# Fused windowed attention and soft mixture of experts: two PSUM tiles for the second layer, first weight tiles cut across four experts, and another grouping of the output rows

## The chip, the cores and the metric

One core of one Trainium2 chip. The metric is the device time of one execution in microseconds (us); before the change it is 223.0 us, the median of three runs (222.9 to 223.66).

## The reference, cut to what matters

```python
x = attention(q, k, v)                # 4 sink keys + a window of 128; x: 3072 tokens x 512
logits = x @ phi                      # 512 -> 32 slots (8 experts x 4 slots)
d = softmax(logits, axis=0);  slot_input = d.T @ x          # 32 x 512
for e in range(8):                    # w1: 8 x 512 x 1024,  w2: 8 x 1024 x 512
    h = np.maximum(slot_input[e] @ w1[e], 0.0)
    slot_out[e] = h @ w2[e]
c = softmax(logits, axis=1)
return c @ slot_out                   # 3072 x 512, fp32
```

All is fp32. The change touches what follows the attention: the two expert layers and the last product.

## The kernel before, in words

A planner (`Plan`) writes down the attention part in an order that it works out from costs and keys. During that part most of the expert weights are loaded into a ring of 22 tiles of 1 MB (`slot()`, name `wt`; two more 1 MB places, `first`, take weights too). What follows, `Moe.tail`, is written out by hand, in program order on each engine, and all its DMAs are issued by SyncE in that order:

- **Layer 1** (lines 634 to 658). Two rounds `r` of four experts. `hp` is a pair of PSUM tiles, one for each half `f` of the 1024 hidden columns. For each quarter `k` of the 512 inputs the four experts' products (`j`, 32 rows of PSUM each) run for `f` = 0 and then for `f` = 1. A weight tile of kind 0 holds two experts' 1024 columns of one quarter, so each tile is read for both `f`. After `k` = 0 and `k` = 1 of each round `more(2)` issues two further weight loads; a load waits until TensorE has done with the tile whose place it takes.
- **Layer 2** (`second`, line 663). `second(r, h, k0, k1)` multiplies the hidden values of round `r` with column half `h` of `w2`. Both halves are summed in one PSUM tile, `op`, of two banks, one for each `h`. The last four loads are `w2` of experts 0 to 3, half 1 (kind 1), which only `second(0, 1)` reads, in turns of `j` = 0 to 3.
- **`split(h)`** (line 673). ScalarE (line 675) and then VectorE (line 676) turn a finished half of `op` into the two-part right operand `tw` of the last product.
- **`combine(h, parts)`** (line 682). The output is 12 row groups `n` (256 tokens each) by two column halves `h`: 24 pieces of 256 KB. A piece is two matmuls, one copy out of PSUM (line 691, ScalarE for even `n`, VectorE for odd) and its part of an output DMA (line 692); each pair in `parts` is one DMA. `combine(0, ...)` is run between parts of `second(1, 1)`, so that output can be written while half 1 is still being computed.

The framework makes an instruction wait by whole tiles: a matmul that writes a PSUM tile waits until what still reads that tile is done.

Of the kernel before, what the change touches and what calls it, by code (L numbers as in the profile page):

```python
# [8 lines left out]
F32 = mybir.dt.float32  # L9
# [10 lines left out]
P = 128  # L20
# [58 lines left out]
class Sinks:  # L79


    def __init__(self, nc, plan, pool, tmp, c, v, store):
# [35 lines left out]
        def project(e):  # L118
            for a in range(4):
                nc.tensor.matmul(M["tile"][:, 0:32], lhsT=per[:, a].rearrange("p b x -> p (b x)"), rhs=c.phi[:, a, :],  # L120
                                 start=(a == 0), stop=(a == 3))

        plan.add(9.5, "D", 2.0, load, w=["v4"])
        plan.add(1.0, "G", 0.6, clear, w=["swide", "vphi", "pst"])
        plan.add(1.0, "G", 0.15, lambda e: nc.gpsimd.tensor_copy(tmp[:, 64:128], v4), r=["v4"], w=["v4b"])
# [183 lines left out]
class Moe:  # L309
# [291 lines left out]
    def tail(self, slot, wts, more, out):  # L601
        nc, c, B, si, pool = self.nc, self.c, self.B, self.si, InOrder(self.pools)
        hs = ht = None

        def halves(o, src):
            for x in range(2):
                i = slice(64 * x, 64 * x + 64)
                nc.tensor.transpose(o[x], src[i], c.ident[i, i])

        def turned(r):  # L610
            tp = [pool.tile() for _ in range(2)]
            for k in range(8):
                halves([t[:, 64 * k:64 * k + 64] for t in tp], hs[:, r, k])
            for j in range(4):
                t, o = tp[j // 2].rearrange("p (k y) -> p k y", k=8), 8 * j + 4 * r + 32 * (j % 2)
                eng = nc.vector.tensor_copy if j % 2 else nc.scalar.copy
                eng(ht[:, :, r, j, :, 4 * r:4 * r + 4], t[:, :, o:o + 4].unsqueeze(2).to_broadcast([P, 8, 4, 4]))

        def turn():
            tp = [pool.tile() for _ in range(2)]  # L620
            for u in range(3):
                cf = self.cs[3, u][1].bitcast(F32).rearrange("p y q e i -> p (y q e i)")
                for i in range(2):
                    o = P * u + 64 * i
                    halves([t[:, o:o + 64] for t in tp], cf[:, P * i:P * i + P])
            for x in range(2):
                if self.sinks:
                    o = self.ct[3][:, :, x].rearrange("p u (i y) -> p u i y", i=2)
                else:
                    o = self.ct[3][:, :, :, 64 * x:64 * x + 64]  # L630
                (nc.scalar.copy if x else nc.vector.tensor_copy)(
                    o, tp[x][:, 0:3 * P].rearrange("p (u i y) -> p u i y", u=3, i=2))

        for r in range(2):
            hp = [pool.tile() for _ in range(2)]
            for k in range(4):
                if r == 1 and k == 3:
                    turned(0)
                for f in range(2):
                    for j in range(4):  # L640
                        o = j % 2 * 1024 + 512 * f
                        nc.tensor.matmul(hp[f][32 * j:32 * j + 32, :], lhsT=si[:, k, :],
                                         rhs=wts[0, 4 * r + j // 2 * 2, k][:, o:o + 512],
                                         start=(k == 0), stop=(k == 3))
                if k < 2:
                    more(2)
            if r == 0:
                hs = slot().rearrange("p (r k m) -> p r k m", r=2, k=8)
                ht = slot().rearrange("p (k r j q i) -> p k r j q i", k=8, r=2, j=4, q=4)
                nc.gpsimd.memset(ht, 0.0)  # L650
            o, (h0, h1) = hs[:, r].rearrange("p k m -> p m k"), (h.rearrange("p (m k) -> p m k", k=8) for h in hp)
            nc.scalar.activation(o[:, 0:64], h0, AF.Relu, scale=self.rz)
            nc.vector.tensor_scalar(o[:, 64:128], h1, 0.0, self.rz, op0=ALU.max, op1=ALU.mult)
            if r == 0:
                self.place(slot(), [3], 3)
                more(1)
                for u in range(3):
                    self.stack(pool, 0, 3, u)

        op = pool.tile("s")[:, :, 0:256]  # L660
        tw = slot().bitcast(F32R)[:, 0:1024].rearrange("p (x m) -> p x m", x=2)

        def second(r, h, k0=0, k1=8):
            for k in range(k0, k1):
                for j in range(4):
                    if r:
                        w = wts[2, 4 + j, k // 4][:, 512 * (k % 4) + 256 * h:512 * (k % 4) + 256 * h + 256]
                    else:
                        w = wts[1, j, h][:, 256 * k:256 * k + 256]
                    nc.tensor.matmul(op[32 * j:32 * j + 32, h], lhsT=ht[:, k, r, j].rearrange("p q i -> p (q i)"), rhs=w,  # L670
                                     start=(r == h and k == 0), stop=(r == 1 - h and k == 7), skip_group_check=True)

        def split(h):
            hi = tw[:, 0, 256 * h:256 * h + 256]
            nc.scalar.copy(hi, op[:, h])  # L675
            nc.vector.scalar_tensor_tensor(tw[:, 1, 256 * h:256 * h + 256], hi.bitcast(F32), c.lo_rows, op[:, h],  # L676
                                           op0=ALU.mult, op1=ALU.add)


        ov = out.rearrange("(n p) m -> p n m", p=P)  # L680

        def combine(h, parts):
            o = slice(256 * h, 256 * h + 256)
            for n0, n1 in parts:
                ob = slot()[:, 0:512 * (n1 - n0)].rearrange("p (n m) -> p n m", m=256)
                for n in range(n0, n1):
                    yp = pool.tile().rearrange("p (i m) -> p i m", i=2)
                    for i in range(2):
                        nc.tensor.matmul(yp[:, i], lhsT=self.ct[n // 3][:, n % 3, i, :], rhs=tw[:, 1, o],
                                         start=(i == 0), stop=(i == 1), skip_group_check=True)  # L690
                    (nc.vector.tensor_copy if n % 2 else nc.scalar.copy)(ob[:, 2 * (n - n0):2 * (n - n0) + 2], yp)  # L691
                nc.sync.dma_start(ov[:, 2 * n0:2 * n1, o], ob)

        second(0, 0, 0, 4)
        turned(1)
        second(0, 0, 4, 8)
        turn()
        second(1, 0)
        split(0)

        second(1, 1, 0, 2)

        combine(0, ((0, 1), (1, 2), (2, 4)))
        second(1, 1, 2, 3)
        combine(0, ((4, 7),))
        second(1, 1, 3, 4)
        combine(0, ((7, 10),))
        second(1, 1, 4, 8)
        second(0, 1)
        split(1)  # L710
        combine(0, ((10, 12),))
        combine(1, ((0, 1), (1, 2), (2, 4), (4, 8), (8, 12)))


class Weights:


    def __init__(self, nc, w1, w2):
        self.nc, self.w1, self.w2, self.tiles, self.at = nc, w1, w2, [], {}
        first = [(0, 4 * r + 2 * j, k) for r in range(2) for k in range(4) for j in range(2)]  # L720
        self.order = first[:8] + [(1, e, 0) for e in range(4)] + first[8:]
        self.order += [(2, e, h) for h in range(2) for e in range(4, 8)] + [(1, e, 1) for e in range(4)]

    def load(self, t):
        kind, e, h = self.order[len(self.tiles)]
        if kind == 0:
            t2, w = t.rearrange("p (k m) -> p k m", k=2), self.w1[e:e + 2].rearrange("e (k p) m -> p e k m", p=P)[:, :, h, :]
        elif kind == 2:
            t2, w = t.rearrange("p (k m) -> p k m", k=4), self.w2[e].rearrange("(p k) m -> p k m", p=P)[:, 4 * h:4 * h + 4]
        else:  # L730
            t2 = t.rearrange("p (k m) -> p k m", k=8)
            w = self.w2[e].rearrange("(p k) m -> p k m", p=P)[:, :, 256 * h:256 * h + 256]
        self.nc.sync.dma_start(t2, w)
        self.tiles.append(t)
        self.at[kind, e, h] = t
# [50 lines left out]
def window_path(ctx, tc, c, moe, q, k, v, phi, w1, w2, out):  # L786
# [299 lines left out]
    for n, (b, j) in enumerate(jobs):  # L1086
# [3 lines left out]
        for kind in range(2):  # L1090
            for i in range(2):
                load(t(O["load"][kind]), n, kind, i)
            prep(t(O["prep"][kind]), n, kind)
        for i in range(2):
            load(t(O["v"][i]), n, 2, i)
# [266 lines left out]
```

## Time and profile before

| | |
|---|---|
| median of three runs | 223.0 us |
| profiled execution | 224.03 us, its span 222.3 us |
| TensorE busy | 201.1 us, 90% of the span |
| layer 1 starts | 171.15 us |
| half 0 of layer 2 complete | 194.3 us |
| half 1 complete (`split(1)` starts) | 206.36 us |
| last copy out of PSUM ends | 212.35 us |

All times are of the profiled execution's span. The 1.7 us between the span and the execution's time lie outside the span. Read first what the DMA engines do in the tail (share and GB/s by stretch), then the chain of waits there.

### The profile page before, as it was taken

How to read it: one execution, taken by the hardware profiler on the slowest of the kernel's cores; microseconds unless marked ns; L12 is line 12 of the kernel's file. 1: busy time of each engine (PE TensorE's matmuls, PEld its weight loads, DVE VectorE, ACT ScalarE, POOL GpSimd, SP SyncE). 2: the span in 40 equal slices, each digit the busy share in tenths (PEclk: the TensorE clock that was granted, in tenths of full speed). 3: DMA queues.
4: the chain of work that ended last, by engine and by line, in shares of the span. 5: the costliest groups of instructions: out<-in, count | busy, mean ns of one | idle time of the engine just before them, and what ended most of it. 6: DMA issues, size and time to landing. Idle time of an engine off the chain costs nothing.

```text
span 222.3 us, 9076 instructions
## 1 busy us (share of the span) xinstructions
PE 201.1 (90%) x3595; PEld 143.8 (65%) x3595; DVE 161.2 (73%) x459; ACT 146.0 (66%) x582; POOL 129.6 (58%) x247
## 2 busy tenths in 40 slices
PE   7977999998999999999999999998999999989800
PEld 6855787776777776776777777766777335555600
DVE  3778898798999989999987989999866123142710
ACT  2456699998888889788998889798445013141600
POOL 5069598877787796578887767877735240000000
PEclk9999999999999999999999999999999999999995
DMA  5998989898999979999999999994479999999696
GB/s 129 222 187 162 177 192 268 209 274 206 220 277 220 336 179 333 245 212 272 219 344 197 261 208 351 382 403 168 191 249 378 379 420 388 356 353 379 225 330 202
DMA packets 95829, 59.47 MB, mean 268 GB/s; under 512 B 76324, under 2 KB 90660, under 8 KB 94756
## 3 DMA queue, kind: packets, MB, share of 16 engines
q1 hardware_dynamic: 95776, 58.83, 91.2%
q8 instruction: 30, 0.49, 1.0%
q14 instruction: 19, 0.16, 0.2%
q10 hardware_dynamic: 4, 0.00, 0.0%
HBM read 52.53 MB, written 6.29 MB: 265 GB/s over the span
## 4 chain that ended last, share of the span: by engine, by line
PE 60%; DVE 15%; ACT 10%; issue 6%; POOL 5%; POOLq 0%; ACTq 0%; DVEq 0%
PE w L155 41%; PE s L155 17%; ACT wt L155 8%; DVE s L155 5%; DVE wt L155 5%; POOL wt L155 5%; DVE sums L155 2%; PE w L1314 2%; DVE rs L155 1%; DVE first L155 1%; DVE acc L155 1%; ACT wt L691 1%; DVE wt L676 0%; ACT wt L675 0%; DVE wt L691 0%
## 5 line engine op out<-in xcount | busy, mean ns | idle before, releaser
L155 ACT ACTIVATE wt<-s,wt 128x132 f32<-128x132 f32 x192 | 68.9, 380 | 9.4 <-DVE wt L155 6.4
L155 POOL TENSOR_TENSOR wt<-wt 128x528 f32<-128x528 f32 x46 | 49.3, 1073 | 18.4 <-DVE wt L155 7.9
L155 POOL TENSOR_SCALAR_AFFINE_SELECT wt<-wt 128x512 f32<-128x512 f32 x84 | 51.1, 636 | 7.4 <-ACT wt L155 3.8
L155 PE MATMUL w<-wt 128*64 128x128 f32 (+2 forms) x548 | 49.9, 316 | 1.9 <-POOL wt L155 1.4
L155 PE MATMUL s<-wt,qt 64*64 64x196 f32 (+2 forms) x768 | 43.0, 326 | 2.4 <-ACT wt L155 1.4
L155 PEld LDWEIGHTS w<-wt 128*64 128x64 f32 (+1 forms) x548 | 35.6, 140 | 14.4 <-POOL wt L155 3.8
L155 ACT ACTIVATION_READ_ACCUMULATOR wt<-s,wt 128x1 f32 x192 | 41.3, 215 | 0.0
L155 DVE TENSOR_REDUCE wt<-s 128x4 f32<-128x528 f32 x48 | 34.0, 708 | 1.7
L155 ACT COPY wt<-w 128x512 f32<-128x512 f32 (+2 forms) x39 | 21.8, 558 | 15.0 <-PE w L155 12.1
L155 PE MATMUL w<-ident,wt 64*128 64x64 f32 (+1 forms) x569 | 28.7, 231 | 1.9 <-POOL wt L155 1.0
L155 PEld LDWEIGHTS s<-wt,qt 64*64 64x64 f32 x768 | 25.4, 133 | 7.6 <-ACT wt L155 2.3
L155 PEld LDWEIGHTS w<-ident,wt 64*128 64x128 f32 (+1 forms) x569 | 22.2, 139 | 10.4 <-issue 4.3
L155 DVE COPY wt<-w 128x512 f32<-128x512 f32 (+2 forms) x36 | 22.8, 654 | 5.4 <-PE w L155 5.0
L155 ACT COPY first<-w 128x512 f32<-128x512 f32 x37 | 21.4, 596 | 3.6 <-PE w L155 3.2
L155 DVE COPY_PREDICATED s<-later,s 128x256 f32<-128x256 uint8 x48 | 20.3, 423 | 2.3 <-PE s L155 1.8
L155 PE MATMUL w<-ident,first 64*128 64x64 f32 x448 | 20.8, 232 | 0.3 <-DVE acc L155 0.2
L155 PEld LDWEIGHTS w<-ident,first 64*128 64x128 f32 x448 | 16.6, 141 | 6.6 <-issue 3.2
L155 PE MATMUL s<-wt 128*32 128x256 f32 x240 | 15.9, 381 | 1.0 <-DVE wt L676 1.0
L155 PE MATMUL w<-wt,si 128*32 128x512 f32 x120 | 14.1, 593 | 0.0
L155 PEld LDWEIGHTS s<-wt 128*32 128x32 f32 x240 | 7.8, 110 | 7.4 <-DVE wt L676 1.5
L155 DVE TENSOR_SCALAR wt<-wt 128x6 f32<-128x6 f32 x48 | 11.5, 240 | 0.7 <-ACT wt L155 0.3
L155 POOL COPY sk<-wt 128x16 f32<-128x16 f32 x48 | 9.4, 208 | 4.2 <-PE w L155 2.6
(134 smaller groups left out, 252.3 us busy)
## 6 DMA issues: line engine op xcount, KB each, us to landing
wt<-in_moe_w_dram SPq DMA_DIRECT2D x30, 1024.0 KB, 8.5
wt<-in_v_dram SPq DMA_DIRECT2D x24, 256.0 KB, 4.4
first<-in_q_dram SPq DMA_DIRECT2D x14, 256.0 KB, 4.3
first<-in_k_dram SPq DMA_DIRECT2D x14, 256.0 KB, 4.6
wt<-in_k_dram SPq DMA_DIRECT2D x8, 256.0 KB, 4.9
wt<-in_q_dram SPq DMA_DIRECT2D x8, 256.0 KB, 5.0
first<-in_moe_w_dram SPq DMA_DIRECT2D x2, 1024.0 KB, 7.0
out_dram<-wt SPq DMA_DIRECT2D x2, 1024.0 KB
```

The source lines that it names most:

```text
L155: return self.tc.keep_in_program_order(f(*args, **kw))
L691: (nc.vector.tensor_copy if n % 2 else nc.scalar.copy)(ob[:, 2 * (n - n0):2 * (n - n0) + 2], yp)
L1314: nc.tensor.matmul(t[:, 0:P], lhsT=c.ident, rhs=c.ident, start=True, stop=True)
```

## The change

Three edits, all in `Moe.tail` and `Weights`:

1. `op` becomes two PSUM tiles, one for each half.
2. The first two weight tiles change their cut: kind 3 holds four experts' quarter `k` = 0 for one half `f` (512 columns each, 2 KB runs) in place of two experts' 1024 columns (4 KB runs). So `f` = 0 reads only the first of them, and a load is issued after each `f`, one and one, in place of two after both. The number of loads and their order behind are as they were (`more(2)` at the three later points).
3. `combine(0, ...)`: four row groups, then 4-6, 6-8 (before: 4-7, 7-10) between the parts of `second(1, 1)`. Behind `split(1)` come 8-10, then half 1's first four, then half 0's 10-12, then half 1's 4-8 and 8-12 (before: half 0's 10-12, then half 1).

```diff
                 for f in range(2):
                     for j in range(4):
                         o = j % 2 * 1024 + 512 * f
-                        nc.tensor.matmul(hp[f][32 * j:32 * j + 32, :], lhsT=si[:, k, :],
-                                         rhs=wts[0, 4 * r + j // 2 * 2, k][:, o:o + 512],
+                        w = wts[3, 0, f][:, 512 * j:512 * j + 512] if r + k == 0 else wts[0, 4 * r + j // 2 * 2, k][:, o:o + 512]
+                        nc.tensor.matmul(hp[f][32 * j:32 * j + 32, :], lhsT=si[:, k, :], rhs=w,
                                          start=(k == 0), stop=(k == 3))
-                if k < 2:
+                    if r + k == 0:
+                        more(1)
+                if 0 < r + k < 3 and k < 2:
                     more(2)
...
-        op = pool.tile("s")[:, :, 0:256]
+        op = [pool.tile("s")[:, 0, 0:256] for _ in range(2)]
...
-        combine(0, ((4, 7),))
+        combine(0, ((4, 6),))
         second(1, 1, 3, 4)
-        combine(0, ((7, 10),))
+        combine(0, ((6, 8),))
         second(1, 1, 4, 8)
         second(0, 1)
         split(1)
+        combine(0, ((8, 10),))
+        combine(1, ((0, 1), (1, 2), (2, 4)))
         combine(0, ((10, 12),))
-        combine(1, ((0, 1), (1, 2), (2, 4), (4, 8), (8, 12)))
+        combine(1, ((4, 8), (8, 12)))
...
-        self.order = first[:8] + [(1, e, 0) for e in range(4)] + first[8:]
+        self.order = [(3, 0, 0), (3, 0, 1)] + first[2:8] + [(1, e, 0) for e in range(4)] + first[8:]
...
+        elif kind == 3:
+            t2 = t.rearrange("p (k m) -> p k m", k=4)
+            w = self.w1[0:4].rearrange("e (k p) m -> p e k m", p=P)[:, :, 0, 512 * h:512 * h + 512]
```

TensorE at the start of layer 1, before the change: `wt_795` and `wt_1034` are the first two weight tiles, `w_3634` and `w_3635` the two halves `f` of `hp`, `si_121` the slot inputs.

```order
L155 MATMUL w_3634<-wt_795,si_121 32x512 [waits DVE_49,Activation_49]
L155 MATMUL w_3634<-wt_795,si_121 32x512
L155 MATMUL w_3634<-wt_1034,si_121 32x512 x2
L155 MATMUL w_3635<-wt_795,si_121 32x512 [waits PE_49]
L155 MATMUL w_3635<-wt_795,si_121 32x512
L155 MATMUL w_3635<-wt_1034,si_121 32x512 x2
```

The same place after it:

```order
L155 MATMUL w_3634<-wt_795,si_121 32x512 [waits DVE_49,Activation_49]
L155 MATMUL w_3634<-wt_795,si_121 32x512 x3
L155 MATMUL w_3635<-wt_1034,si_121 32x512 [waits PE_49]
L155 MATMUL w_3635<-wt_1034,si_121 32x512 x3
L155 MATMUL w_3634<-wt_1306,si_121 32x512 x2
```

The first tile's last reader is now the fourth of the eight matmuls, where it was the sixth; the second tile's is the eighth in both.

TensorE where half 0 of layer 2 ends and half 1 begins, before the change: `s_3756` is `op`, `wt_3656` to `wt_3682` are the last weights of half 0, `wt_3540` and the rows behind it begin `second(1, 1)`.

```order
L155 MATMUL s_3756<-wt_3656,wt_3677 32x256
L155 MATMUL s_3756<-wt_3658,wt_3677 32x256
L155 MATMUL s_3756<-wt_3682,wt_3677 32x256
L155 MATMUL s_3756<-wt_3540,wt_3677 32x256 [waits DVE_49]
L155 MATMUL s_3756<-wt_3631,wt_3677 32x256
L155 MATMUL s_3756<-first1_77,wt_3677 32x256
```

The same place after it, with `s_3756` and `s_3757` the two tiles of `op`:

```order
L155 MATMUL s_3756<-wt_3656,wt_3677 32x256
L155 MATMUL s_3756<-wt_3658,wt_3677 32x256
L155 MATMUL s_3756<-wt_3682,wt_3677 32x256
L155 MATMUL s_3757<-wt_3540,wt_3677 32x256
L155 MATMUL s_3757<-wt_3631,wt_3677 32x256
L155 MATMUL s_3757<-first1_77,wt_3677 32x256
```

The wait on VectorE (for `split(0)`) is gone from the first matmul of half 1.

TensorE from the first `combine` to its last, before the change: `s` rows are `second`, `w` rows are `combine` (two matmuls to a row group; those that read `qt` are row groups 6 to 8).

```order
L155 MATMUL w<-wt 128x256 x4
L155 MATMUL w<-wt,qt 128x256 x2
L155 MATMUL s<-wt 32x256 x2
L155 MATMUL s<-first_77,wt 32x256
L155 MATMUL s<-wt 32x256
L155 MATMUL w<-wt,qt 128x256 x4
L155 MATMUL w<-wt 128x256 x2
L155 MATMUL s<-wt 32x256 x48
L155 MATMUL w<-wt 128x256 x16
L155 MATMUL w<-wt,qt 128x256 x6
L155 MATMUL w<-wt 128x256 x6
```

The same place after it:

```order
L155 MATMUL w<-wt 128x256 x4
L155 MATMUL s<-wt 32x256 x2
L155 MATMUL s<-first_77,wt 32x256
L155 MATMUL s<-wt 32x256
L155 MATMUL w<-wt,qt 128x256 x4
L155 MATMUL s<-wt 32x256 x48
L155 MATMUL w<-wt,qt 128x256 x2
L155 MATMUL w<-wt 128x256 x18
L155 MATMUL w<-wt,qt 128x256 x6
L155 MATMUL w<-wt 128x256 x6
```

Two row groups (8 and 9) have moved from before the 48 matmuls to behind them, so 16 pieces stand behind `split(1)` where 14 did.

## Rows read from the trace of the kernel before

**Rows 1.** The page: the span, and busy time by engine (us, share, instructions).

```profile
span 222.3 us, 9076 instructions
PE 201.1 (90%) x3595; PEld 143.8 (65%) x3595; DVE 161.2 (73%) x459; ACT 146.0 (66%) x582; POOL 129.6 (58%) x247
```

**Rows 2.** Stretches: us, busy PE, PEld, DVE, ACT, POOL; granted clock, DMA share, GB/s.

```profile
174.00:175.00 1.00, 1.00 (x12) 0.31 (x8) 0.00 (x0) 0.00 (x0) 0.00 (x0) 1.00 1.14 369
175.00:176.00 1.00, 1.00 (x16) 0.44 (x12) 0.00 (x0) 0.00 (x0) 0.00 (x0) 1.00 0.81 287
176.00:177.00 1.00, 1.00 (x16) 0.34 (x11) 0.00 (x0) 0.00 (x0) 0.44 (x1) 1.00 1.01 369
177.00:178.00 1.00, 1.00 (x12) 0.31 (x8) 0.00 (x0) 0.57 (x1) 1.00 (x1) 1.00 0.96 401
178.00:186.00 8.00, 8.00 (x92) 3.08 (x88) 1.70 (x4) 1.99 (x4) 2.40 (x7) 1.00 1.00 418
200.00:206.00 6.00, 5.99 (x100) 3.30 (x98) 1.24 (x2) 0.59 (x1) 0.00 (x0) 1.00 1.08 379
206.00:209.00 3.00, 2.69 (x17) 2.01 (x16) 2.00 (x4) 2.03 (x4) 0.00 (x0) 1.00 0.34 121
209.00:219.00 10.00, 2.38 (x14) 1.72 (x14) 3.04 (x5) 2.28 (x4) 0.00 (x0) 0.84 1.04 338
219.00:222.30 3.30, 0.00 (x0) 0.00 (x0) 0.00 (x0) 0.00 (x0) 0.00 (x0) 0.50 0.28 96
```

**Rows 3.** Chain that ended last, 193 to 223 us: start us, us, what.

```profile
192.93 1.34 PE s L155 x24
...
194.29 0.38 ACT wt L675
...
194.69 0.49 DVE wt L676
...
195.23 1.07 PE s L155 x16
196.30 1.14 PE w L155 x8
...
198.01 0.90 PE w L155 x6
...
199.48 0.91 PE w L155 x6
200.39 2.29 PE s L155 x38
...
202.68 3.65 PE s L155 x58
...
206.36 0.38 ACT wt L675
...
206.76 0.49 DVE wt L676
...
207.30 1.69 PE w L155 x10
...
211.66 0.69 DVE wt L691
```

**Rows 4.** Weight-load timeline, 201.5 to 204: start, us, engine, instruction, count [idle, releaser].

```profile
202.68 1.24 PEld L155 LDWEIGHTS s<-wt 128*32 128x32 f32 x28 [0.49 <-DMA wt<-in_moe_w_dram]
```

**Rows 5.** Timeline of TensorE, 171.1 to 180 us.

```profile
171.15 8.79 PE L155 MATMUL w<-wt,si 128*32 128x512 f32 x80
```

**Rows 6.** Timeline of SyncE's DMA issues, 168 to 173.4 us.

```profile
168.71 0.33 SPq L155 DMA_DIRECT2D first<-in_moe_w_dram  x1
173.09 0.33 SPq L155 DMA_DIRECT2D wt<-in_moe_w_dram  x1
```

**Rows 7.** Timeline of SyncE's DMA issues, 207 to 213 us.

```profile
207.91 5.02 SPq L692 DMA_DIRECT2D out_dram<-wt  x6
```

**Rows 8.** Waits of TensorE's weight loads, whole run: us in total, times, longest.

```profile
PEld s L155 <- DMA wt<-in_moe_w_dram: 0.5, 1, 0.5
...
PEld w L155 <- DMA wt<-in_moe_w_dram: 0.3, 1, 0.3
```

More of the change, by code (lines that the diff above doesn't have):

```diff
@@ L669, in second @@
                         w = wts[1, j, h][:, 256 * k:256 * k + 256]
-                    nc.tensor.matmul(op[32 * j:32 * j + 32, h], lhsT=ht[:, k, r, j].rearrange("p q i -> p (q i)"), rhs=w,
+                    nc.tensor.matmul(op[h][32 * j:32 * j + 32], lhsT=ht[:, k, r, j].rearrange("p q i -> p (q i)"), rhs=w,
                                      start=(r == h and k == 0), stop=(r == 1 - h and k == 7), skip_group_check=True)
@@ L674, in split @@
             hi = tw[:, 0, 256 * h:256 * h + 256]
-            nc.scalar.copy(hi, op[:, h])
-            nc.vector.scalar_tensor_tensor(tw[:, 1, 256 * h:256 * h + 256], hi.bitcast(F32), c.lo_rows, op[:, h],
+            nc.scalar.copy(hi, op[h])
+            nc.vector.scalar_tensor_tensor(tw[:, 1, 256 * h:256 * h + 256], hi.bitcast(F32), c.lo_rows, op[h],
                                            op0=ALU.mult, op1=ALU.add)
```

## Prediction

> **What bounds the kernel now.** I read three views, in this order. The page says that TensorE is busy for 90% of the 222.3 us [rows 1]; that is an average, and the change lies in the last 50 us, so I read that stretch by itself. The stretches of the tail [rows 2] show a second bound there: the DMA engines. Their share is about 1 in every stretch shown from 174 to 206 us but one, first on weights, then also on output. From 206 to 209 us it falls to 0.34: the output pieces computed so far are written, and half 1's do not exist yet. From 209 to 219 us the share is 1.04 again, at 338 GB/s, while TensorE works only 2.4 of the 10 us. So the end is set by a drain: 14 pieces of 262 kB (3.67 MB) that start to flow at about 209 us, and 3.67 MB / 338 GB/s = 10.9 us. An edit gains only if the drain starts earlier or has less to write.
>
> What sets its start? The chain [rows 3] goes back from 209: the first DMA behind `split(1)` is issued at 207.91 [rows 7], which is 1.55 us after the split begins at 206.36, and data flows at full share 1.1 us after that. Before the split TensorE works through 58 passes (an fp32 matmul is two) from 202.68 on. There the weight loads stood idle for 0.49 us, released by a weight's DMA [rows 4]: the last weight tile, the one for `j` = 3 of `second(0, 1)`. So the last weight opens the end: 202.68 + 3.65 (58 passes) + 2.65 = about 209. TensorE itself was hardly ahead of it: it can have lost no more than those 0.49 us, and since its 38 passes before took 2.29 us, 0.060 each, and the 58 behind 0.063 each [rows 3], no gap shows in the chain; I take 0.2, the middle.
>
> **The change part by part.**
>
> *Two PSUM tiles.* Half 0 is complete at 192.93 + 1.34 = 194.27; TensorE then waits for ScalarE (0.38) and VectorE (0.49) and starts half 1 at 195.23 [rows 3]. With two tiles the 16 passes of `second(1, 1, 0, 2)`, 1.07 us, run in that time. The second tile is the other buffer of a pool of two, which nothing else uses in the tail, so opening it waits for nothing. The first `combine` row now carries the wait for VectorE (done at 195.18), but its 16 passes end at 194.27 + 1.07 = 195.3, so the wait is covered. `combine` starts at 195.3, not 196.30: TensorE gains 1.0 us.
>
> *Row groups 8 and 9 behind the split.* Three row groups cost 0.90 and 0.91 us [rows 3], so two cost 0.6. TensorE comes to the last weight 1.0 + 0.6 = 1.6 us earlier, and with the 0.2 that it waited there already, the split can start up to 1.8 us earlier. It does so only if the last weight is there. The two pieces do not vanish: they stand in the drain, 2 x 262 kB / 338 GB/s = 1.55 us more to write. Before, they were written while the DMA engines were busy anyway, from 200 to 206 us; now the queue simply runs dry earlier, by 0.52 MB / 379 GB/s = 1.4 us. Behind the split the 16 pieces are computed faster than they drain: the last of the 14 was copied by 211.66 + 0.69 = 212.35 [rows 3], 6 us behind the split, against 10.9 us of writing, so computing two more is hidden by the drain. Of SyncE's queue: the output DMAs keep their place behind all weight loads; the first one behind the split is now that of 8-10, with the same two copies in front of it as 10-12 had, and 10-12 goes past half 1's first three. Each waits only for its own copies, and while the drain lasts nobody waits for SyncE.
>
> *The first two tiles by halves.* Eight of the 16 passes of `k` = 0 take 8 x 8.79/80 = 0.88 us [rows 5], so the first reload can be issued at about 172.2 in place of 173.09 [rows 6]; the second stays near 173.1. What this is worth is seen right behind: the load before was issued at 168.71, and from 174 to 178 us the rate was 369, 287, 369 and 401 GB/s against 418 in the eight us after [rows 2]; in the second of these the DMA engines were idle for a fifth of their time. The shortfall is 49 + 131 + 49 + 17 = 246 kB per us of 418, or 0.6 us of the whole stream. With a load already waiting I expect most of that back, and since the share stays at 1 from there to 206 us, the last weight would land about 0.6 us earlier. The bounds are 0 (the shortfall has another cause, or the slowest engine does not share in it) and 1.8 (the slowest engine was the one that stood idle, and gets back more than the mean; more than 1.8 is of no use to TensorE).
>
> The trace shows a share over all 16 engines, and one wait that ended when the last of them was done. The Trainium skill, page "DMA: Bandwidth & Descriptors", section "Why a DMA increments its semaphore by 16 and not by 1", says that the engines of a DMA finish independently and only the full count means that the data is there. By that rule the 0.6 us of the mean is not what TensorE sees, and both of my bounds stay open; the rows cannot narrow it, since no view names the engine.
>
> The loading of these two tiles, during attention, is cut into 2 KB runs. The trace has no such load: by the slowest rate of the tail, 338 GB/s, a tile of 1.05 MB costs 3.1 us, by the fastest, 418, 2.5 us; so between 0 and 0.6 us each. TensorE's weight loads waited for a DMA twice in the whole run, 0.5 and 0.3 us, both times for expert weights [rows 8], never for the attention's inputs, which those tiles stand beside in SyncE's queue. So the lead of these inputs covers it and I take 0, with 0.6 as the bound if one of them becomes late.
>
> *One DMA more* (12, the two of 768 kB cut to three of 512 kB). From 200 to 206 us pieces of this kind were written at a share of 1.08 [rows 2], without a gap between DMAs, so I take 0. The same page of the Trainium skill asks in "Rules for kernel authors" for at least 1 MiB in a DMA, and in "Anatomy of one DMA" it gives about 2.0 us of fixed cost for each (for those that GpSimd issues). As an estimate by that page, one more DMA standing exposed would make the sum below +2.35 in place of +0.35 us; the row of full share speaks against it, since a DMA that is followed by the next in the queue exposes nothing.
>
> **The sum.** Let D be how much earlier the split starts, 0 to 1.8 us. The end moves by 1.55 - D. With D = 0.6 it is +0.95, with D = 1.8 it is -0.25; I take the middle, D = 1.2, since the engine that stood idle is likely to be the late one: +0.35 us. On the profiled execution's 224.03 us that gives 224.4; the median of the runs lies 1.0 us lower, and I put the same step on it: 223.0 + 0.35 = 223.3 us. So TensorE's gain of 1.6 us is mostly spent: a part waits for the weight, and the rest is paid back by the two pieces moved into the drain.
>
> **The rivals.** A difference under 0.5% (1.1 us) can't be told from none here.
>
> - *The last weight lands where it did* (slower). The shortfall at 175 us came from something else, or the slowest engine is slow later on. Then D is 0 to 0.4, TensorE stands for about 1.6 us before the 58 passes, and the drain has 1.55 us more: 224.1 to 224.6, at D = 0 it is 224.5. For it: TensorE already waited there. Against it: the dip lies exactly behind the late reload. It decides from D below 0.45.
> - *The drain is faster* (faster). While reads and writes were mixed the rate was 379 GB/s, later 338 [rows 2]. If the drain with 16 pieces goes at 379, it takes 4.19 MB / 379 = 11.1 us, only 0.2 more than the 10.9 of before, and D of 1.2 to 1.8 stays as a gain of 1.0 to 1.6: 221.4 to 222.0. For it: half 0 and half 1 now alternate in the drain. Against it: the 338 is held for ten microseconds at full share, with nothing but output in the queue.
> - *The 2 KB loads delay attention* (no gain, or slower). One early load is late by up to 0.6 us and TensorE with it, on top of +0.35: 223.9. Against it: the loads lie many microseconds ahead of layer 1.
>
> **How the numbers follow.** The forecast with D from 0.5 to 1.8 has 0.48, from 222.7 to 224.0; the late weight 0.22; the faster drain 0.20; the late attention 0.10. Faster by more than 0.5% (below 221.9) holds three quarters of the faster drain: 0.15. Slower (above 224.1) holds nearly all of the late weight and a part of the last case: 0.25. The rest, 0.60, is within 0.5%. The range that leaves out about 2 in 10 is 222.0 to 224.6.
>
> **What would show it.** In the profile after: no wait for line 676 at the first matmul of half 1, and `combine` about 1.0 us earlier; the first reload issued near 172.2, and no dip at 175 us; a wait for a weight's DMA in front of the 58 passes that is longer than 0.49 us, as long as D is under 1.8; a stretch of low DMA share that starts about a microsecond and a half before 206; and behind it a drain of about 12.4 us at about 338 GB/s. I am wrong if the weight wait is gone and the drain still starts no earlier, if the drain is clearly faster than 338 GB/s, or if layer 1 no longer starts 171 us after the beginning.

## The result, and the profile after

The changed kernel takes 225.34 us (median of six runs, 224.89 to 225.54); beside it on the same chip the kernel before took 223.26 us (six runs, 222.9 to 223.7). The ratio is 1.0089, with a 95% interval of 1.0071 to 1.0108: slower by 2.1 us. The forecast was 223.3 us and its range ended at 224.6. The profiled execution took 225.45 us.

A part of each time lies outside the span: 1.7 to 1.9 us in the runs of before, 2.05 to 2.2 in those of the changed kernel. The medians of the spans are 223.25 us for the changed kernel and 221.3 to 221.5 for the 91 runs of before that were taken beside the experiments below. So of the 2.1 us about 1.75 lie in the span, and 0.35 outside it.

The page of after, against [rows 1]:

```profile
span 223.4 us, 9077 instructions
PE 200.4 (90%) x3595; PEld 143.0 (64%) x3595; DVE 161.5 (72%) x459; ACT 146.2 (65%) x582; POOL 129.9 (58%) x247
```

No engine's busy time moves by more than 0.8 us. The time is in the gaps. The stretches of after, columns as in [rows 2]:

```profile
174.00:175.00 1.00, 1.00 (x16) 0.41 (x12) 0.00 (x0) 0.00 (x0) 0.00 (x0) 1.00 1.24 328
175.00:176.00 1.00, 1.00 (x16) 0.38 (x12) 0.00 (x0) 0.00 (x0) 0.00 (x0) 1.00 0.73 221
176.00:177.00 1.00, 1.00 (x12) 0.31 (x8) 0.00 (x0) 0.00 (x0) 0.55 (x1) 1.00 0.96 352
177.00:178.00 1.00, 1.00 (x16) 0.40 (x12) 0.00 (x0) 0.68 (x1) 1.00 (x1) 1.00 0.92 369
178.00:186.00 8.00, 8.00 (x92) 3.03 (x88) 1.82 (x4) 1.97 (x4) 2.30 (x7) 1.00 1.01 419
200.00:206.00 6.00, 4.76 (x79) 2.42 (x69) 0.00 (x0) 0.00 (x0) 0.00 (x0) 1.00 0.99 347
206.00:209.00 3.00, 2.69 (x18) 2.26 (x18) 2.36 (x4) 2.37 (x5) 0.00 (x0) 1.00 0.25 87
209.00:219.00 10.00, 2.68 (x16) 1.90 (x14) 3.31 (x6) 2.60 (x5) 0.00 (x0) 0.86 1.04 337
219.00:222.30 3.30, 0.00 (x0) 0.00 (x0) 0.00 (x0) 0.00 (x0) 0.00 (x0) 0.50 0.66 219
```

Three things are to be seen. TensorE is idle for 1.24 of the six us from 200 to 206, where it was idle for 0.01. The drain runs at the same 337 GB/s and is simply longer: the last stretch, which carried 96 GB/s before, carries 219. And the dip at 175 us, which the second edit was to fill, is still there: 328, 221, 352 and 369 GB/s against 419 leave 91 + 198 + 67 + 50 = 406 kB per us missing, about 1.0 us of the stream.

The chain of waits of after (start us, us, what), against [rows 3]:

```profile
189.84 12.44 DMA wt<-in_moe_w_dram
202.28 0.04 issue
202.33 3.65 PE s L155 x58
...
206.00 0.38 ACT wt L677
...
206.41 0.49 DVE wt L678
...
206.94 1.69 PE w L155 x10
...
211.26 1.30 DVE wt L693 x2
```

Before, the chain went back through TensorE to half 0 of layer 2; now it leaves TensorE at 202.33 and goes through the last weight load alone. (The new lines stand two further down: line 677 is 675 of before.) The timelines of TensorE, ScalarE and SyncE's DMA issues in after (start us, us, engine, instruction, count, and in brackets the idle time ahead and its releaser):

```profile
171.05 8.79 PE L155 MATMUL w<-wt,si 128*32 128x512 f32 x80
...
172.16 0.33 SPq L155 DMA_DIRECT2D wt<-in_moe_w_dram  x1
...
195.12 1.21 PE L155 MATMUL w<-wt 128*128 128x256 f32 x8
...
198.73 2.36 PE L155 MATMUL s<-wt 128*32 128x256 f32 x38
...
202.33 3.64 PE L155 MATMUL s<-wt 128*32 128x256 f32 x58 [1.24 <-DMA wt<-in_moe_w_dram]
...
206.00 0.37 ACT L677 CAST wt<-s 128x256 fp32r<-128x256 f32 x1 [6.82 <-PE s L155]
...
207.56 6.39 SPq L694 DMA_DIRECT2D out_dram<-wt  x7
```

`combine` begins at 195.12 where it began at 196.23, and the last 96 passes at 198.73 where they began at 200.32. (These are the starts in the timeline; the chain of [rows 3] has 196.30 and 200.39 for before.) Then TensorE waits 1.24 us for the last weight. In the timeline of before, the 96 passes stand in one row, since there TensorE itself shows no idle time:

```profile
200.32 6.01 PE L155 MATMUL s<-wt 128*32 128x256 f32 x96
```

### The profile page after: what moved, and what is told of

Read it like the earlier page. It is cut to its first block, busy times and chain, and to the rows that moved or that the text cites. A ratio compares the mean times of both kernels' runs of the same rounds, so it can differ in the third digit from the quotient of the medians.

```text
span 223.4 us, 9077 instructions
## 1 busy us (share of the span) xinstructions
PE 200.4 (90%) x3595; PEld 143.0 (64%) x3595; DVE 161.5 (72%) x459; ACT 146.2 (65%) x582; POOL 129.9 (58%) x247
## 4 chain that ended last, share of the span: by engine, by line
PE 49%; DVE 16%; DMA 9%; ACT 8%; POOL 7%; issue 6%; ACTq 0%; DVEq 0%; POOLq 0%
PE w L155 37%; PE s L155 12%; POOL wt L155 7%; ACT wt L155 6%; DMA wt<-in_moe_w_dram 6%; DVE s L155 5%; DVE wt L155 5%; DMA wt<-in_v_dram 3%; DVE sums L155 2%; DMA ints<-in_window_dram 1%; DVE rs L155 1%; DVE wt L693 1%; DVE first L155 1%; DVE acc L155 1%; ACT wt L693 1%
```

## The experiments

In each, the kernel before was timed on the same chip. "Split" is the start of ScalarE's copy in `split(1)`, "pieces" are those computed behind it, and the drain is the span's end minus the issue of the first output DMA behind the split. A weight has landed with the last increment of its DMA's semaphore, as the trace records it.

**A second profile of before.** No edit.

> The kernel before, unchanged, for a second profile of it. Theory A (the last weight and TensorE open the end together): the split starts between 205.3 and 206.4 us, with no or a short wait (under 0.5 us) for the last weight, and the drain of 14 pieces takes about 10.9 us. If the first profile was a late one, the split is about 1 us earlier and the span about 1 us shorter. Other theories: no difference to the first profile.

One execution of 222.91 us, span 221.2; 23 further runs of before beside it have a median of 223.06. Its timelines:

```profile
170.62 8.79 PE L155 MATMUL w<-wt,si 128*32 128x512 f32 x80
...
199.79 5.39 PE L155 MATMUL s<-wt 128*32 128x256 f32 x96
...
205.25 0.37 ACT L675 CAST wt<-s 128x256 fp32r<-128x256 f32 x1 [5.00 <-PE s L155]
...
206.80 5.08 SPq L692 DMA_DIRECT2D out_dram<-wt  x6
```

All 96 passes run through in 5.39 us: no wait for the last weight. In this execution it lands at 201.46 us, only 0.1 before TensorE turns to the 39th pass, the first that reads it (its weight load starts at 201.56); in the first profile of before it landed at 202.64 and the split was at 206.36 [rows 3]. So that profile, 224.03 us in a kernel whose median is 223.0 to 223.3, showed a late weight, and this one is the better base. Two more kernels below keep TensorE's pace of before, edit 2 alone and the other order; neither waits, with 0.3 and 0.9 us to spare.

Against this profile the changed kernel's span is 2.2 us longer: the split 0.75 later (206.00 for 205.25), the first DMA as far behind it (1.56 for 1.55), and the drain 15.84 us for 14.40, 1.44 more. Of the 0.75, 0.43 is there when layer 1 starts: at 171.05 in the changed kernel, at 170.62 here.

**Each edit alone.** Edit 1:

```diff
-        op = pool.tile("s")[:, :, 0:256]
+        op = [pool.tile("s")[:, 0, 0:256] for _ in range(2)]
...
```

> Edit 1 alone (a PSUM tile for each half). Theory A (the last weight opens the end, and what stands behind the split is written at the drain's rate): TensorE comes 1.0 us earlier to the last weight and waits there, 1.0 to 1.3 us in place of at most 0.5; the split starts at most 0.2 us earlier; time -0.2 to 0 us against before. Theory B (the cut in 2 KB runs costs the time): the same, 0. Theory C (the second PSUM tile itself costs): +1 to +2 us.

Measured 223.27 us, ratio 0.9988 (0.9965 to 1.0010). Edit 2 (of its code only the order of the tiles is shown):

```diff
-        self.order = first[:8] + [(1, e, 0) for e in range(4)] + first[8:]
+        self.order = [(3, 0, 0), (3, 0, 1)] + first[2:8] + [(1, e, 0) for e in range(4)] + first[8:]
...
```

> Edit 2 alone (first two weight tiles by four experts, a load after each half). Theory A: the first reload is issued 0.9 us earlier, the last weight lands 0 to 0.4 us earlier; time -0.2 to 0 us. Theory B: the early loads or the cut cost: +1 to +2 us, the layers start later than 171.1 us or the last weight lands later. Theory C: 0.

Measured 223.35 us, 1.0004 (0.9975 to 1.0033). Edit 3:

```diff
-        combine(0, ((4, 7),))
+        combine(0, ((4, 6),))
...
-        combine(0, ((7, 10),))
+        combine(0, ((6, 8),))
...
+        combine(0, ((8, 10),))
+        combine(1, ((0, 1), (1, 2), (2, 4)))
         combine(0, ((10, 12),))
-        combine(1, ((0, 1), (1, 2), (2, 4), (4, 8), (8, 12)))
+        combine(1, ((4, 8), (8, 12)))
```

> Edit 3 alone (row groups 8 and 9 behind the split). Theory A: the split starts at most 0.2 us earlier, 16 pieces in place of 14 stand in the drain, 1.55 us more: +1.3 to +1.6 us. Theory B and theory C: 0, or -0.6 us by the two row groups that TensorE no longer does ahead of the split.

Measured 225.06 us, 1.0068 (1.0041 to 1.0095). Edits 1 and 2 together, with before's grouping:

> Edits 1 and 2 without 3. Theory A: TensorE is 1.0 us early at the last weight, which lands 0 to 0.4 us earlier; 14 pieces in the drain as before: -0.4 to 0 us. Theory B: +1 to +2 us. Theory C: +1 to +2 us.

Measured 223.31 us, 0.9997 (0.9972 to 1.0023). So the third edit alone costs 1.5 us by the ratio, and for the other two neither a gain nor a loss can be told. (By the medians of the spans, edit 1 alone and edits 1 and 2 together are 0.3 us shorter than before, which the noise covers, and edit 3 alone is 1.4 longer; the rest lies outside the span.) The timelines say why a faster TensorE brings nothing. With edit 1 alone:

```profile
201.64 3.64 PE L155 MATMUL s<-wt 128*32 128x256 f32 x58 [0.24 <-DMA wt<-in_moe_w_dram]
...
205.32 0.37 ACT L675 CAST wt<-s 128x256 fp32r<-128x256 f32 x1 [5.81 <-PE s L155]
```

With edit 3 alone:

```profile
202.97 3.64 PE L155 MATMUL s<-wt 128*32 128x256 f32 x58 [1.40 <-DMA wt<-in_moe_w_dram]
...
208.19 6.43 SPq L692 DMA_DIRECT2D out_dram<-wt  x7
```

Counted from the start of layer 1, TensorE begins the 96 passes 29.17 us behind it in both profiles of before, 28.17 with edit 1, 28.70 with edit 3 and 27.68 with all three: it saves 1.0, 0.5 and 1.5 us. Each time it then stands in front of the last weight, and the stop costs more than its idle time. The 96 passes take 5.39 us where they run through; they take 6.01 in the first profile of before, 6.24 with edit 1 and 7.24 with all edits, where TensorE's own idle time is 0, 0.24 and 1.24. That is 0.6 us more than the idle time in each.

The profile with edit 3 alone is of a late execution (226.05 us, one above that kernel's median). Its stretches show the other half of the price: next to nothing to write from 206 to 209, and the last stretch nearly full.

```profile
206.00:209.00 3.00, 2.68 (x20) 1.89 (x15) 1.72 (x4) 1.83 (x4) 0.00 (x0) 1.00 0.08 27
...
219.00:222.30 3.30, 0.00 (x0) 0.00 (x0) 0.00 (x0) 0.00 (x0) 0.00 (x0) 0.50 0.85 282
```

And the dip: with edit 2 alone, whose reload is issued at 172.08 us, the rate is

```profile
174.00:175.00 1.00, 1.00 (x16) 0.43 (x12) 0.00 (x0) 0.00 (x0) 0.00 (x0) 1.00 0.97 213
175.00:176.00 1.00, 1.00 (x15) 0.31 (x8) 0.00 (x0) 0.00 (x0) 0.00 (x0) 1.00 0.89 303
```

and with edits 1 and 2, where layer 1 has the same code, it is

```profile
174.00:175.00 1.00, 1.00 (x16) 0.46 (x12) 0.00 (x0) 0.00 (x0) 0.00 (x0) 1.00 1.05 401
175.00:176.00 1.00, 1.00 (x16) 0.33 (x11) 0.00 (x0) 0.00 (x0) 0.00 (x0) 1.00 0.98 393
```

The second profile of before, with the late reload at 172.56, has 328 and 401. The dip comes and goes whether the reload is early or not. Nor does the last weight land earlier: counted from the start of layer 1 it lands after 30.1 to 31.3 us in the five profiles with edit 2 and the uncut last weights (mean 30.8) and after 30.1 to 32.4 in the five without edit 2 (mean 31.1).

Edit 2 also reaches into the attention. The weight-load timeline near 59 us, in the first profile of before:

```profile
59.20 1.28 PEld L155 LDWEIGHTS w<-wt 128*64 128x64 f32 x16 [0.28 <-POOL vphi L155]
```

With edit 2 alone:

```profile
59.39 0.85 PEld L155 LDWEIGHTS w<-wt 128*64 128x64 f32 x12 [0.87 <-DMA wt<-in_v_dram]
```

With all edits:

```profile
59.45 0.85 PEld L155 LDWEIGHTS w<-wt 128*64 128x64 f32 x12 [0.66 <-DMA wt<-in_v_dram]
```

All seven profiles of kernels with edit 2 show such a wait for an input of the attention at this place, 0.5 to 0.9 us; of the seven without it only one does, 0.2 us. (At other places four of these seven wait once for such an input, 0.3 to 0.7 us.) The load waited for took 5.1 to 5.7 us from issue to landing with edit 2, and 3.2 to 3.3 in six of the seven without. Layer 1 starts at 170.96 to 171.59 us with edit 2 (mean 171.1) and at 170.50 to 171.15 without (mean 170.8), so some 0.3 us may be the price of the early loads. The times can't tell it: the interval of edit 2 alone goes from -0.6 to +0.7 us.

**More and fewer pieces in the drain.** All edits, with 6-8 behind the split too (18 pieces):

```diff
-        combine(0, ((6, 8),))
...
-        combine(0, ((8, 10),))
+        combine(0, ((6, 8), (8, 10)))
```

> The changed kernel with two more row groups (6 and 7) moved behind the split: 18 pieces there. Theory A: TensorE waits for the last weight 0.6 us longer, the split does not move, the drain has 1.55 us more: +1.5 us against the changed kernel, +3.3 to +3.7 us against before. Rival (the cost of the change lies in the two groups 8 and 9 or in the order of the output DMAs, not in their number): the same time as the changed kernel, about +1.9 us against before.

Measured 226.51 us, 1.0173 (1.0125 to 1.0221); TensorE waits 0.86 us for the weight, the drain is 17.87 us, 2.0 more than with 16 pieces. Its median is 3.45 us above before's, as expected, and 1.2 above the changed kernel's, where 1.5 was expected; so the number of pieces counts, and not only groups 8 and 9. Edits 1 and 2 with all of half 0 ahead of the split (12 pieces):

```diff
+        combine(0, ((10, 12),))
...
         split(1)
-        combine(0, ((10, 12),))
```

> Edits 1 and 2, and row groups 10 and 11 of half 0 too ahead of the second part of half 1: no piece of half 0 behind the split, 12 pieces there. Theory A: TensorE has 0.4 to 0.7 us to spare at the last weight, so the split moves by 0 to 0.2 us; the first piece behind it comes 0.2 to 0.5 us later, as it has to wait for the split; the drain has 1.55 us less: -0.6 to -1.3 us against before. Rival (the row groups behind the split are needed there to cover TensorE's wait for the split): 0 to +0.6 us.

Measured 222.89 us, 0.9993 (0.9964 to 1.0022). This one missed: a gain of 0.6 to 1.3 us was expected. Its timelines:

```profile
202.29 3.16 PEld L155 LDWEIGHTS s<-wt 128*32 128x32 f32 x58 [0.50 <-DMA wt<-in_moe_w_dram]
...
205.97 0.37 ACT L677 CAST wt<-s 128x256 fp32r<-128x256 f32 x1 [3.87 <-PE s L155]
...
208.06 4.33 SPq L694 DMA_DIRECT2D out_dram<-wt  x5
```

The drain is 1.76 us shorter than with 14 pieces (12.64 for 14.40). But the first DMA is 1.26 us later than in the second profile of before (208.06 for 206.80). It now comes 2.09 us behind the split, not 1.55, since nothing of half 0 is left to compute while ScalarE and VectorE work. And the split is 0.7 later: layer 1 began 0.34 later (170.96), and TensorE, which is early by edit 1 and has two more row groups to do, still met a late weight (landed at 202.25; the first line is the wait). What is left of the gain, 0.55 us by the medians of the spans (220.75 for 221.3), is in part made up outside the span.

**The order behind the split.** Before, with half 1's first four ahead of 10-12:

```diff
         split(1)
+        combine(1, ((0, 1), (1, 2), (2, 4)))
         combine(0, ((10, 12),))
-        combine(1, ((0, 1), (1, 2), (2, 4), (4, 8), (8, 12)))
+        combine(1, ((4, 8), (8, 12)))
```

> The kernel before with only the order behind the split changed: half 1's first four row groups go ahead of half 0's 10 to 12; 14 pieces there as before. Theory A: the number of pieces is the same, the first comes 0.2 to 0.5 us later: +0.2 to +0.5 us. Rival (alternating halves in the drain change its rate): the rate from 209 to 219 us is off 338 GB/s by more than 3%, time off by more than 0.5 us either way.

Measured 223.92 us, 1.0041 (1.0024 to 1.0059): 0.9 us slower, where 0.2 to 0.5 was expected. The split is at 205.12, the first DMA at 207.22, again 2.10 behind, which is 0.55 of the 0.9; the profiled execution, the fastest of ten (223.47 us), doesn't show the rest:

```profile
205.12 0.37 ACT L675 CAST wt<-s 128x256 fp32r<-128x256 f32 x1 [4.99 <-PE s L155]
...
207.22 4.96 SPq L692 DMA_DIRECT2D out_dram<-wt  x6
```

The drain went at 335 GB/s from 209 to 219 us, so alternating halves does not speed it. In the changed kernel 8-10 stands ahead of half 1 and the DMA comes 1.56 behind the split, so this 0.55 is not in its sum.

**The last weight taken away.** All edits, without the last weight load (what is left out: expert 3's half 1 of `w2` is neither loaded nor used; expert 2's stands in for it):

```diff
-                        w = wts[1, j, h][:, 256 * k:256 * k + 256]
+                        w = wts[1, min(j, 3 - h), h][:, 256 * k:256 * k + 256]
...
-                    more(2)
+                    more(2 - (r + k == 2))
```

> The changed kernel without the last weight load: the half-1 weights of expert 3 are not loaded, and expert 2's are used in their place, so one 1 MB read and the wait for it are left out of the computation; TensorE's work is the same. Theory A: TensorE no longer waits before the last 58 passes, the split starts 1.2 to 1.5 us earlier than in the changed kernel, and so does the drain: -1.2 to -1.5 us against it, +0.5 to +0.9 us against before. Rival (the wait is harmless, the end is set by all of the DMA traffic or by the copies): within 0.3 us of the changed kernel.

Measured 223.70 us, 1.0020 (1.0001 to 1.0039), 1.6 us less than the changed kernel, where 1.2 to 1.5 was expected. TensorE runs all 96 passes through and the split is at 204.33:

```profile
198.88 5.39 PE L155 MATMUL s<-wt 128*32 128x256 f32 x96
...
205.89 6.38 SPq L694 DMA_DIRECT2D out_dram<-wt  x7
```

This also takes 1 MB from the DMA engines; the next experiment does not.

**The last weights cut another way.** The last four tiles hold two of the eight `k` for all four experts each, so that 16 passes and not 58 stand behind the last to land. The bytes are the same; each tile is two DMAs of 512 KB.

```diff
-                        w = wts[1, j, h][:, 256 * k:256 * k + 256]
+                        w = wts[1, j, 0][:, 256 * k:256 * k + 256] if h == 0 else wts[4, 0, k // 2][:, 1024 * (k % 2) + 256 * j:1024 * (k % 2) + 256 * j + 256]
...
+        elif kind == 4:
+            t3, w3 = t.rearrange("p (k j m) -> p k j m", k=2, j=4), self.w2[0:4].rearrange("e (p k) m -> p k e m", p=P)
+            self.nc.sync.dma_start(t3[:, 0], w3[:, 2 * h, :, 256:512])
+            t2, w = t3[:, 1], w3[:, 2 * h + 1, :, 256:512]
```

With edit 1 and the grouping of before:

> Edit 1, and the last four weight tiles cut across the experts: each holds two of the eight hidden eighths for all four experts (two DMAs of 512 KB), so behind the last landing 16 passes remain in place of 58. Groups as before the change. Theory A: TensorE keeps its 1.0 us, the split starts at about 204.2 us, the drain has 14 pieces: -0.7 to -1.0 us against before. Rival (the end is set by all of the DMA traffic): 0.

Measured **222.51 us, 0.9962 (0.9946 to 0.9978)**: faster than both kernels. With all of half 0 ahead of the split as well:

> The recut with edit 1, and all twelve row groups of half 0 ahead of the split: 12 pieces behind it. Theory A: the split starts at about 204.8 us, the first piece behind it comes 0.55 us later than with the cover of 10 to 12, the drain is 1.55 us shorter: -1.2 to -1.5 us against before. Rival (the end is set by all of the DMA traffic): 0; rival (the cover is needed): worse than the recut alone.

Measured 222.55 us, 0.9967 (0.9948 to 0.9987). With all three edits:

> The changed kernel (all three edits) with the last four weight tiles cut across the experts. Theory A: TensorE's 1.6 us show at last, the split starts at about 203.6 us, 16 pieces stand behind it: -1.7 to -2.2 us against the changed kernel, -0.2 to +0.4 us against before. Rival (the wait for the weight is harmless): within 0.3 us of the changed kernel.

Measured 223.79 us, 1.0011 (0.9995 to 1.0028), 1.55 less than the changed kernel, where 1.7 to 2.2 was expected; by the medians of the spans it is 1.2 (222.05 for 223.25). The timelines of the first:

```profile
198.81 5.39 PE L155 MATMUL s<-wt 128*32 128x256 f32 x96
...
204.27 0.37 ACT L675 CAST wt<-s 128x256 fp32r<-128x256 f32 x1 [4.99 <-PE s L155]
...
205.82 5.12 SPq L692 DMA_DIRECT2D out_dram<-wt  x6
```

And of the third:

```profile
198.69 5.39 PE L155 MATMUL s<-wt 128*32 128x256 f32 x96
...
205.69 6.38 SPq L694 DMA_DIRECT2D out_dram<-wt  x7
```

Neither waits. The third is the cleanest test: its last weight's last increment comes at 202.78 us, later than the changed kernel's, and still the first DMA behind the split is issued 1.87 us earlier (205.69 for 207.56), since so little work stands behind that weight. These two kernels differ in edits 2 and 3 only, the weight gates neither, and the drains are 14.68 and 16.11 us: two pieces cost 1.43 us. The middle one missed its expected gain of 1.2 to 1.5 us, with 0.7. Its first DMA behind the split and its stretches:

```profile
207.58 4.35 SPq L692 DMA_DIRECT2D out_dram<-wt  x5
...
206.00:209.00 3.00, 2.48 (x15) 2.07 (x16) 2.17 (x4) 1.93 (x4) 0.00 (x0) 1.00 1.01 354
209.00:219.00 10.00, 1.61 (x10) 1.15 (x9) 2.17 (x4) 1.45 (x3) 0.00 (x0) 0.67 0.96 321
```

The first DMA comes 1.76 us later than in the first of the three (207.58 for 205.82), and the drain is as much shorter, 12.92 us for 14.68. No dry stretch is left, so what is moved ahead of the split seems only to take another's turn: as far as these two profiles show, the bytes set the end there.

**Outside the span.** The changed kernel's 0.35 us there is not the price of an edit. 1.65 to 1.9 us lie outside the span in all runs of before, edit 2 alone, the 18 pieces, the other order and the recut with all edits; 2.0 to 2.25 in all runs of the changed kernel and the other seven. All three edits stand in kernels of both kinds. What makes the difference was not found; it has the size of several effects above, so the spans are given beside the times where it matters.

## Why the prediction was wrong

- **How much earlier the split starts** (D): this is the step that failed. It took 1.2 us, the middle of 0.6 and 1.8, "since the engine that stood idle is likely to be the late one". Measured from the first profile of before, D is 0.36 (206.36 to 206.00); from the second, which is the nearer to the median, it is -0.75, of which 0.43 is the later layer 1. TensorE came 1.5 us earlier to the last weight, and its stop there cost 1.85 (7.24 us for 5.39).
- **The reason given for D**, that the late reload made the dip and the dip the late weight: fell. The reload came at 172.16, as predicted, the dip stayed, and the last weight landed where it did, within its scatter.
- **The bound D of 0 or more**: too narrow, through the choice of the base. The 0.49 us of [rows 4] was read as the usual state. It was one late landing: of the four profiles at before's pace only that one waits. In the second profile, which is near the median, the weight was 0.1 us ahead of TensorE, and a landing up to that point cost nothing. Once TensorE comes 1.5 us sooner, each landing goes through to the end. The forecast put the step of a late execution on a median that was not late.
- **The wait in before, put at 0.2 us**: it cost 0.6. The prediction saw no gap, since the 38 and the 58 passes took about as long each; but 96 passes that run through take 5.39 us, and there they took 6.01.
- **TensorE's gain** (1.0 + 0.6 us): right, at 1.0 + 0.5.
- **The two pieces** (+1.55 us): right, at 1.43 and 1.44 us; the two from 16 to 18 cost 2.0, the two from 12 to 14 1.76.
- **One DMA more, put at nothing**: right as far as the drain shows it, which goes at 337 GB/s as before.
- **The 2 KB loads, put at nothing**: not right. The prediction took the lead of the attention's inputs to cover them, and an input was late in every profile with edit 2. Some 0.3 us of later layer 1 would fit, within the 0.6 that it gave as the bound; no time shows it.
- **The rivals.** "The last weight lands where it did" came true, had 0.22, and ended at 224.6, since its D stopped at 0. The faster drain fell by the 337 and 335 GB/s. The late attention came true in kind; edit 2 alone (1.0004) leaves no room for more than 0.7 us of it.

The split's 0.75 and the drain's 1.44 us add up to 2.2, the difference of the two spans. That this is close to the 2.1 between the medians is in part luck. The medians of the spans differ by about 1.75. So in the usual execution the drain's 1.44 leaves about 0.3 for a later split, and the 2.1 us of the times hold 0.35 that lies outside the span and in no term of the prediction.

The share of all 16 engines could not tell when the slowest would be done. The Trainium skill, page "DMA: Bandwidth & Descriptors", section "Why a DMA increments its semaphore by 16 and not by 1", says that the engines of one DMA finish independently. The trace agrees: in the changed kernel the increments of the last load run from 200.03 to 202.28 us, and TensorE goes on at 202.33, behind the last.

What stays open: whether the third edit itself makes the weight land later. It landed at 202.28 and 202.92 us in the two profiles with 16 pieces and uncut last weights, but at 201.66 with 18, and with 14 anywhere from 200.56 (the other order) to 202.64 (the first profile of before); one execution each doesn't part this from scatter. Nor was it found what makes the dip at 175 us, what lies outside the span, or how much of the 2.1 us the late input of edit 2 has.

## What to carry to other kernels

Before an engine ahead of a wait is made faster, ask which of the two arrivals is late in most executions: a second profile of the same kernel costs one run, and here it would have taken away the base of the sum. Where a last load gates the end, cut the last tiles so that little work stands behind the last one to land; here that made the saved time count (0.8 us less than before in all) and took the scatter of the landing off the path (with edit 1, ten runs from 222.30 to 222.95 us, where before has 222.61 to 224.66). A load with time to spare for itself may still make its neighbours in the queue late: see who waits for those. Work moved behind the point where the output queue runs dry is paid in full: two pieces are 1.55 us by their bytes at the drain's 338 GB/s, and cost 1.4 to 2.0.

## What the runs showed of the hardware

The landing of a load that SyncE issues in the same place differs from execution to execution by more than an edit was worth: the last weight was issued at 189.87 and done at 201.46 us in the second profile of before, 189.99 and 201.59 with edit 1, 189.84 and 202.28 in after, 191.07 and 202.64 in the first profile of before, 190.97 and 202.92 with edit 3. The last of its 16 increments came 1.7 to 3.7 us behind the first, over the ten profiles that have this load. A stop of TensorE in the middle of 96 passes cost 0.6 us beside its idle time, in each of six profiles. And from 174 to 176 us the rate lay anywhere from 213 to 426 GB/s in a microsecond, with the loads of layer 1 in the same order.
